# Sparse attention and a rational feed-forward layer on one core: two of nine chunks evaluate their polynomials from h squared and leave two sums to accumulating transfers, the magnitudes of b come later, and every engine has a new order

## The chip, the cores and the metric

One core of a Trainium2 chip. The metric is the device time of one execution in microseconds (us); the figure for a kernel is the median of its runs. The profile of one execution gives a span, from its first to its last instruction, and the time of that execution lies a little above its span.

## The reference, cut to what matters

Eight batches, eight heads, 576 positions, head dimension 64. Four heads see the last 32 positions, four see every 32nd position. The result x (4608 tokens by 512) goes through a layer whose activation is a quotient of polynomials:

```python
attn = softmax(where(mask[h], q @ k.T / 8, -1e9))
x = (attn @ v)                        # (4608, 512)
h = x @ w_in                          # (4608, 2048)
P = a[0] + a[1]*h + a[2]*h*h + a[3]*h*h*h
Q = 1.0 + abs(b[0])*abs(h) + abs(b[1])*h*h
out = (P / (Q + 1e-6)) @ w_out        # (4608, 512)
```

## The kernel before, in words

The program is one flat list of operations. `graph` records each of them with its tiles, `P.op` derives what it must wait for, and five lists of numbers, `ORDER`, say in which order each engine runs them; `AT` places the PSUM banks. Nothing is decided at run time. An engine works strictly down its list, so an instruction that waits holds up all that stand behind it in that list.

Attention runs batch by batch (`attention`, b = 0 to 7). GpSimd's queue casts q, k and v (`casts`), SyncE's queue loads and transposes them from batch 2 on (`loads`, L464 to L492), TensorE (PE) computes scores, VectorE (DVE) the row maxima and sums (L637, L666, L748), ScalarE (ACT) the exponentials (L661, L764, L767), and ACT evicts the result into XT, the transposed x (L413, called from L838 and L888). For batch 0 the sums of the strided softmax are L666, their reciprocal L668.

The feed-forward layer runs in nine chunks of 512 tokens (`mlp`, c = 0 to 8; the "chunks 7 and 8" of the change are c = 6 and 7 here). Per chunk, PE computes 16 blocks of 128 features (`w1`, L907), ACT evicts each into h (L918), and a group of up to 8 blocks, 128 x 4096 elements in bf16, is then evaluated at once:

- |h| into z, on ACT (L934) or on DVE (L938);
- Q: u = |b1|z + |b0| (L941), u = u z (L944), on DVE;
- 1/Q as exp(-ln(1 + u)), two halves each on ACT (L948, L953);
- P by Horner's rule in z on DVE: L957, L960, L962, L964, L966;
- h = z u (L968), on DVE.

PE then multiplies h by w_out (`w2`, L984), in pieces of four matmuls, ACT evicts (L992) and SyncE's queue stores (L998). Chunks 0 to 7 have groups of 8 blocks (chunk 0: 4, 4, 8), chunk 8 has 8, 4, 2, 2. The groups of a chunk are counted from 0, so "group 6,1" is the second of chunk 6. In the table MLP (L1033) chunk 6 has |h| on ACT in both groups, chunk 7 on ACT in its first and on DVE in its second.

The magnitudes |b0|, |b1| are one small DVE instruction (`babs`, L317) behind two small loads that ACT's queue issues (L314). Matmuls on constants (`fill`, L306) keep PE at work: 10 at the start, 5 in batch 0, 12 before the last products of chunk 8. Zeros are written by DVE (L327) and by ACT (L329), the latter as 0.0 times a column of the constants, which must have landed first.

## Time and profile before

| | |
|---|---|
| median of 3 runs | 373.1 us (367.28 to 377.19) |
| the profiled execution | 368.85 us, span 367.0 us, mean granted clock 0.963 |
| busy: PE, DVE, ACT | 324.5, 321.5, 318.8 us (88, 88, 87%) |
| busy: GpSimd (POOL) | 55.0 us (15%) |
| DMA engines | 0.5 to 1.0 busy up to about 240 us, then 0.0 to 0.2 in the slices of the page |

How to read it: three engines are equally busy over the whole, so the sums alone do not tell which bounds. What an engine waited for is in brackets behind a row of the timeline, with the wait in us. A row of the timeline merges neighbours of one kind ("x39"), and a row's duration includes the first instruction's start-up, so that two DVE or ACT instructions that follow each other overlap a little in these rows: what one costs in a full queue is the distance between the starts.

### The profile page before, as it was taken

The page shows a single profiled execution, that of the slowest core. Times are in us where ns is not written, and L with a number is a line of the kernel's source. Part 1 is how long each engine was busy: PE and PEld are TensorE (multiplying, and loading weights), DVE is VectorE, ACT ScalarE, POOL GpSimd, SP SyncE. Part 2 cuts the span into 40 slices and gives each one's busy share as a digit, 9 for nine tenths or more (in the row PEclk, how much of TensorE's full clock was granted, in tenths as well). Part 3 has the DMA queues.
Part 4 walks back from the last instruction along what each step waited for, and adds up shares of the span by engine and source line. Part 5 has one row for each costly group of instructions (what it writes and reads, how often), then busy time and mean ns, then how long its engine had stood idle before and what let it go on. Part 6 is the DMA issues. An engine that isn't in the chain of part 4 may idle for free.

```text
span 367.0 us, 9362 instructions
## 1 busy us (share of the span) xinstructions
PE 324.5 (88%) x4173; PEld 163.9 (45%) x4221; DVE 321.5 (88%) x272; ACT 318.8 (87%) x372; POOL 55.0 (15%) x90
## 2 busy tenths in 40 slices
PE   5669987779989995999999988999999799999795
PEld 2445544434544543445444544454454344444342
DVE  6961999998999995769998999799899969999991
ACT  7646798968999995599999999989999999999872
POOL 8893000240050014000600310000000000000000
PEclk9896999969999997899999999999999899999999
DMA  9999999688969959967999899810202010100202
GB/s 153 201 154 179 216 200 169 113 161 139 199 147 205 187 85 170 190 144 146 159 197 196 178 147 210 146 72 17 63 3 59 30 57 0 59 29 29 86 30 114
DMA packets 93080, 46.24 MB, mean 126 GB/s; under 512 B 79376, under 2 KB 86160, under 8 KB 92560
## 3 DMA queue, kind: packets, MB, share of 16 engines
q1 hardware_dynamic: 77168, 27.27, 38.1%
q0 software_dynamic: 14400, 18.07, 32.2%
q8 instruction: 33, 0.54, 0.6%
q10 hardware_dynamic: 1472, 0.30, 0.6%
q14 instruction: 7, 0.06, 0.1%
HBM read 38.58 MB, written 18.28 MB: 155 GB/s over the span
## 4 chain that ended last, share of the span: by engine, by line
ACT 40%; PE 31%; DVE 21%; issue 4%; DMA 3%; ACTq 0%
PE ps L907 14%; PE ps L984 12%; ACT u L948 10%; ACT u L953 8%; ACT h L918 8%; ACT z L934 6%; DVE u L944 3%; DVE z L960 3%; ACT XT L413 3%; DVE h L968 2%; DVE z L964 2%; DMA coef<-in_moe_a_dram 2%; DVE u L941 2%; DVE z L957 2%; ACT os L992 1%
## 5 line engine op out<-in xcount | busy, mean ns | idle before, releaser
L907 PE MATMUL ps<-XT,Win 128*128 128x512 bf16 x555 | 132.9, 386 | 8.1 <-ACT XT L413 5.5
L984 PE MATMUL ps<-Wout,h 128*128 128x512 bf16 x549 | 132.6, 386 | 6.3 <-issue 3.1
L918 ACT ACTIVATE h<-ps 128x512 bf16<-128x512 f32 x144 | 79.4, 622 | 16.5 <-PE ps L907 16.4
L907 PEld LDWEIGHTS ps<-XT,Win 128*128 128x128 bf16 x576 | 55.3, 99 | 72.5 <-issue 6.2
L984 PEld LDWEIGHTS ps<-Wout,h 128*128 128x128 bf16 x576 | 54.7, 99 | 66.8 <-issue 3.6
L948 ACT ACTIVATE u<-u 128x2048 bf16<-128x2048 bf16 (+1 forms) x40 | 68.7, 1751 | 1.7 <-DVE u L944 1.5
L953 ACT ACTIVATE u<-u 128x2048 bf16<-128x2048 bf16 (+1 forms) x40 | 69.5, 1759 | 0.1
L934 ACT ACTIVATE z<-h 128x2048 bf16<-128x2048 bf16 (+1 forms) x28 | 47.2, 1746 | 1.9 <-DVE h L968 1.7
L968 DVE TENSOR_TENSOR h<-z,u 128x4096 bf16<-128x4096 bf16 (+2 forms) x21 | 41.6, 1979 | 0.6
L944 DVE TENSOR_TENSOR u<-u,z 128x4096 bf16<-128x4096 bf16 (+2 forms) x21 | 41.6, 1983 | 0.4
L960 DVE TENSOR_TENSOR z<-z,h 128x4096 bf16<-128x4096 bf16 (+2 forms) x21 | 41.5, 1978 | 0.3
L964 DVE TENSOR_TENSOR z<-z,h 128x4096 bf16<-128x4096 bf16 (+2 forms) x21 | 41.5, 1976 | 0.3
L941 DVE TENSOR_SCALAR u<-z,coef 128x4096 bf16<-128x4096 bf16 (+2 forms) x21 | 24.8, 1180 | 7.5 <-ACT z L934 7.5
L400 POOL DMA_DIRECT2D vS<-in_v_dram x32 | 22.9, 722 | 37.6 <-DMA vL<-vL 27.3
L992 ACT ACTIVATE os<-ps 128x512 f32<-128x512 f32 x36 | 21.5, 627 | 7.1 <-PE ps L984 7.1
L957 DVE TENSOR_SCALAR z<-h,coef 128x4096 bf16<-128x4096 bf16 (+2 forms) x21 | 24.9, 1187 | 0.3
L966 DVE TENSOR_SCALAR z<-z,coef 128x4096 bf16<-128x4096 bf16 (+2 forms) x21 | 23.7, 1128 | 0.2
L962 DVE TENSOR_SCALAR z<-z,coef 128x4096 bf16<-128x4096 bf16 (+2 forms) x21 | 23.5, 1118 | 0.1
L413 ACT ACTIVATE XT<-ps 128x576 bf16<-128x576 bf16 (+5 forms) x36 | 20.2, 615 | 1.5 <-PE ps L882 1.4
L362 POOL DMA_DIRECT2D qk<-in_k_dram x12 | 6.3, 523 | 87.3 <-DMA vL<-vL 87.3
L803 PEld LDWEIGHTS ps<-ptS,vS 18*64 18x64 bf16 x896 | 9.1, 106 | 10.4 <-issue 6.4
L803 PE MATMUL ps<-ptS,vS 18*64 18x18 bf16 x896 | 11.4, 175 | 2.2 <-DVE xl L870 1.2
(95 smaller groups left out, 255.0 us busy)
## 6 DMA issues: line engine op xcount, KB each, us to landing
out_dram<-os SPq DMA_DIRECT2D x36, 256.0 KB, 2.2
qk<-in_q_dram POOLq DMA_DIRECT2D x12, 288.0 KB, 7.4
qk<-in_k_dram POOLq DMA_DIRECT2D x12, 288.0 KB, 6.9
vS<-in_v_dram POOLq DMA_DIRECT2D x32, 72.0 KB, 9.3
Win<-in_moe_w_in_dram POOLq DMA_DIRECT2D x2, 1024.0 KB, 12.6
Wout<-in_moe_w_out_dram POOLq DMA_DIRECT2D x2, 1024.0 KB, 20.9
v<-in_v_dram POOLq DMA_DIRECT2D x6, 288.0 KB, 7.6
vL<-v SPq DMA_DIRECT2D x24, 72.0 KB, 4.0
```

Of the source, the lines that this page charges most:

```text
L907: r = e.matmul(bank(ph, 0, CH), Win[:, kk, f * 128:(f + 1) * 128], XT[:, kk, c * CH % NR:c * CH % NR + CH], start=(kk == 0), stop=(kk == N ...
L918: P.op("act", lambda e, f=f, ph=ph, h=h, f0=f0: e.activation(h.t[:, f - f0, :], bank(ph, 0, CH), AF.Copy), "ev512", ("hev", c, f), r=[ph], ...
L934: P.op("act", lambda e, z=z, h=h, i=i, hp=hp: e.activation(z.t[:, hp * i:hp * i + hp, :], h.t[:, hp * i:hp * i + hp, :], AF.Abs), f"act_{h ...
L941: dv(lambda e, z=z, u=u, G_=G_: e.tensor_scalar(u.t[:, 0:G_, :], z.t[:, 0:G_, :], b1_ap, b0_ap, op0=Alu.mult, op1=Alu.add), "ts2", "u1", r ...
L944: dv(lambda e, z=z, u=u, G_=G_: e.tensor_tensor(u.t[:, 0:G_, :], u.t[:, 0:G_, :], z.t[:, 0:G_, :], op=Alu.mult), "tt", "u2", r=[z], m=[u])
L948: lns.append(P.op("act", lambda e, u=u, i=i, hp=hp: e.activation(u.t[:, hp * i:hp * i + hp, :], u.t[:, hp * i:hp * i + hp, :], AF.Ln, bias ...
L953: exs.append(P.op("act", lambda e, u=u, i=i, hp=hp: e.activation(u.t[:, hp * i:hp * i + hp, :], u.t[:, hp * i:hp * i + hp, :], AF.Exp, sca ...
L957: dv(lambda e, z=z, h=h, G_=G_: e.tensor_scalar(z.t[:, 0:G_, :], h.t[:, 0:G_, :], a_ap[3], a_ap[2], op0=Alu.mult, op1=Alu.add), "ts2", "p1 ...
L960: dv(lambda e, z=z, h=h, G_=G_: e.tensor_tensor(z.t[:, 0:G_, :], z.t[:, 0:G_, :], h.t[:, 0:G_, :], op=Alu.mult), "tt", "p2", r=[h], m=[z])
L964: dv(lambda e, z=z, h=h, G_=G_: e.tensor_tensor(z.t[:, 0:G_, :], z.t[:, 0:G_, :], h.t[:, 0:G_, :], op=Alu.mult), "tt", "p4", r=[h], m=[z])
L968: dv(lambda e, z=z, h=h, u=u, G_=G_: e.tensor_tensor(h.t[:, 0:G_, :], z.t[:, 0:G_, :], u.t[:, 0:G_, :], op=Alu.mult), "tt", "g", r=[z, u], ...
L984: r = e.matmul(bank(po, 0, Fout), h.t[:, j, m * 128:(m + 1) * 128], Wout[:, kk, :], start=(kk == 0), stop=(kk == NF - 1))
```

## The change

Four things are changed.

1. Chunks 6 and 7 (`ADDED`) are evaluated by `chain_added`. With t = |b0||h| (ACT takes the factor along as `scale`; DVE needs one more instruction) DVE computes u = h h, s = a3 h + a2, z = a1 h + a0, s = s u and u = |b1| u. The two sums u + t and z + s are made by `into`: a transfer from GpSimd's queue between tiles on chip that adds to its destination, one per sum and group, eight in all, 1 MB each (128 rows of 2 x 2048 elements). ln and exp on u and the product h = z u follow as before. s, t and a third u lie over the tiles of q, k and v, which are free after the attention of batch 7; both chunks are therefore recorded behind it.
2. `babs` is recorded after batch 0's attention and waits for its `lnorm` (L870 of before).
3. ACT's zeros are copied from a column of zeros that DVE writes, and no longer wait for the constants.
4. Fills: 6 behind the first turn of q, 8 behind `lneg` of batch 0 (5 before), 8 behind `snorm` of batch 0. And all five orders and the banks are new; of these tables the diff shows two lines.

```diff
-    QK = [sb(f"qkT{i}", [128, 3 * W]) for i in range(2)]
+    QK_ = sb("qkT", [128, 6 * W])
+    QK = [QK_[:, 3 * W * i:3 * W * i + 3 * W] for i in range(2)]
...
+    L = [Tile(f"l{i}", x[:, o:o + G * CH].rearrange("p (g c) -> p g c", g=G)) for i, (x, o) in enumerate(
+        ((QK_, 0), (VL_, 0), (VL_, NV2), (QK_, G * CH), (QK_, 2 * G * CH)))]
+    R_s, R_t, R_u3 = Ring(L[0:2]), Ring(L[2:4]), Ring(R_u.tiles + L[4:5])
...
+    def babs():
+        last = [o for o in P.ops if o.lab == ("lnorm", 0)]
         P.op("dve", lambda e: e.scalar_tensor_tensor(coef[:, 6:8], coef[:, 4:6], -1.0, coef[:, 4:6],
-                                                     op0=Alu.mult, op1=Alu.max), "tiny", ("babs",), r=[T_co], w=[T_b])
+                                                     op0=Alu.mult, op1=Alu.max), "tiny", ("babs",), r=[T_co], w=[T_b],
+             after=last)
...
+    P.op("dve", lambda e: e.memset(zc[:, :], 0.0), "tiny", ("zc",), w=[T_zc])
...
-            P.op("act", lambda e: e.activation(o(), src, AF.Copy, scale=0.0), kind, lab, r=[T_id], w=[t])
+            P.op("act", lambda e: e.activation(o(), src, AF.Copy), kind, lab, r=[T_zc], w=[t])
...
+                    if (b, nm, pair) == (0, "ql", 0):
+                        fill(6, 3, [o])
...
+        if two:
+            fill(8, 4, [o])
...
-            fill(5, 1, [o])
+            fill(8, 1, [o])
...
+    def into(dst, src, nm, c, gi):
+        if not hasattr(dst, "ac"):
+            dst.ac = Tile("a" + dst.name)
+        dst.ac.new()
+        W = G * CH
+        o = P.op("pool", lambda e: e.dma_start(dst.t.rearrange("p g c -> p (g c)"), src.t.rearrange("p g c -> p (g c)"),
+                                               accum_op=Alu.add, max_dma_last_dim=4096), "issue", (nm, c, gi),
+                 r=[src], w=[dst.ac], after=dst.prev + dst.w + dst.r, dma=(256, 300))
+        dst.w, dst.r = [o], []
...
+    def chain_added(c, gi, h, G_, on_act):
+        u, z, s, t = R_u3.next(), R_z.next(), R_s.next(), R_t.next()
...
+        if on_act:
+            for i in range(2):
+                P.op("act", lambda e, i=i: e.activation(t.t[:, 4 * i:4 * i + 4, :], h.t[:, 4 * i:4 * i + 4, :], AF.Abs,
+                                                        scale=b0_ap), f"act_{W // 2}", ("abs", c, gi, i), r=[h, T_b], w=[t])
+        else:
+            dv(lambda e: e.tensor_scalar(t.t.bitcast(u16)[:, :, :], h.t.bitcast(u16)[:, :, :], 0x7FFF, None,
+                                         op0=Alu.bitwise_and), "ts1", "absd", r=[h], w=[t])
+            dv(lambda e: e.tensor_scalar(t.t[:, :, :], t.t[:, :, :], b0_ap, None, op0=Alu.mult), "ts1", "u0", r=[T_b],
+               m=[t])
+        dv(lambda e: e.tensor_tensor(u.t[:, :, :], h.t[:, :, :], h.t[:, :, :], op=Alu.mult), "tt", "u1", r=[h], w=[u])
+        dv(lambda e: e.tensor_scalar(s.t[:, :, :], h.t[:, :, :], a_ap[3], a_ap[2], op0=Alu.mult, op1=Alu.add), "ts2", "p1",
+           r=[h, T_co], w=[s])
+        dv(lambda e: e.tensor_scalar(z.t[:, :, :], h.t[:, :, :], a_ap[1], a_ap[0], op0=Alu.mult, op1=Alu.add), "ts2", "p2",
+           r=[h, T_co], w=[z])
+        dv(lambda e: e.tensor_tensor(s.t[:, :, :], s.t[:, :, :], u.t[:, :, :], op=Alu.mult), "tt", "p3", r=[u], m=[s])
+        dv(lambda e: e.tensor_scalar(u.t[:, :, :], u.t[:, :, :], b1_ap, None, op0=Alu.mult), "ts1", "u2", r=[T_b], m=[u])
+        into(u, t, "ua", c, gi)
+        into(z, s, "za", c, gi)
...
+        dv(lambda e: e.tensor_tensor(h.t[:, :, :], z.t[:, :, :], u.t[:, :, :], op=Alu.mult), "tt", "g", r=[z, u], m=[h])
...
+            if c in ADDED:
+                chain_added(c, gi, h, G_, abs_act[gi])
+                groups.append((f0 - G_, G_, h))
+                continue
...
+        if b == 0:
+            babs()
...
+        if b == B - 1:
+            qs = [R.tiles[i] for R in (R_sqk, R_lq, R_lk) for i in range(2)]
+            L[0].over, L[3].over, L[4].over = qs, qs, qs
+            L[1].over, L[2].over = [R_vL.tiles[0]], R_vL.tiles[0:2]
-        while nxt < NCH and (nxt + 1) * CH <= (b + 1) * S:
+        while nxt < NCH and (nxt + 1) * CH <= (b + 1) * S and (nxt < ADDED[0] or b == B - 1):
...
+ADDED = (6, 7)
...
-        "20 13 21 11 26 12 24 19 29 23 27 22 31 34 14 30 33 69 32 72 86 75 65 90 93 79 92 142 82 125 151 49 "
+        "27 14 24 15 20 13 22 12 25 23 33 30 75 21 11 92 96 71 78 34 28 32 85 31 35 81 99 98 88 156 131 134 "
...
```

How the order moves, at the three places on which a number of the prediction rests. A row has the line, the operation, and output<-inputs with their buffer numbers; in the changed kernel the line numbers are its own.

DVE in the attention of batch 0, before: L317 is `babs`, L666 and L668 are the sum and the reciprocal of the strided softmax.

```order
L637 TENSOR_REDUCE ng0<-ps 128x32
L413 COPY ptL0<-ps 128x512
L317 SCALAR_TENSOR_TENSOR coef<-coef 128x2
L666 TENSOR_REDUCE rc0<-h1 128x32
L413 COPY qkT1<-ps 64x576
```

And now (L652 and L681 are the same two reductions, L324 is `babs`):

```order
L652 TENSOR_REDUCE ng0<-ps 128x32
L681 TENSOR_REDUCE rc0<-h1 128x32
L426 COPY ptL0<-ps 128x512
L683 RECIPROCAL rc0<-rc0 128x32
L684 TENSOR_TENSOR h1<-h1,rc0 128x2x16x18
L884 RECIPROCAL rc1<-ps 128x18
L887 TENSOR_TENSOR xl0<-ps,rc1 128x1152
L426 COPY h1<-ps 128x512 x2
L426 COPY qkT<-ps 128x576
L324 SCALAR_TENSOR_TENSOR coef<-coef 128x2
```

`babs` stood ahead of the sum; now it stands behind all of batch 0's normalizations.

ACT between chunk 6's first evictions and chunk 7's, before: L934 is |h| of chunk 6, L948 and L953 are ln and exp of its groups, L413 into XT are the evictions of batch 7, on which chunk 7's first matmul waits.

```order
L934 ACTIVATE z<-h 128x2048 x2
L948 ACTIVATE u<-u 128x2048 x2
L953 ACTIVATE u<-u 128x2048
L413 ACTIVATE XT<-ps 128x576
L953 ACTIVATE u<-u 128x2048
L992 ACTIVATE os<-ps 128x512
L948 ACTIVATE u<-u 128x2048 x2
L413 ACTIVATE XT<-ps 128x576 x2
L953 ACTIVATE u<-u 128x2048 x2
L918 ACTIVATE h<-ps 128x512
```

And now (L987 evicts into h, L1065 the output, L934 is |b0||h|, L952 and L956 are ln and exp, L426 evicts into XT):

```order
L934 ACTIVATE vL<-h,coef 128x2048 x2
L987 ACTIVATE h<-ps 128x512
L1065 ACTIVATE os<-ps 128x512
L426 ACTIVATE XT<-ps 128x576 x2
L1065 ACTIVATE os<-ps 128x512
L987 ACTIVATE h<-ps 128x512
L426 ACTIVATE XT<-ps 128x576
L987 ACTIVATE h<-ps 128x512
L426 ACTIVATE XT<-ps 128x576
L934 ACTIVATE qkT<-h,coef 128x2048 x2
L987 ACTIVATE h<-ps 128x512 x3
L952 ACTIVATE u<-u 128x2048
```

All four evictions of batch 7 now stand ahead of chunk 6's first ln; three evictions of chunk 7 do, too, and the rest of chunk 7's stand behind it.

DVE at the first group of chunk 6, now (L681 to L684 are batch 7's softmax; L941, L942, L944, L946, L947 are u, s, z, s and u of `chain_added`; L884 and L887 batch 7's last normalization):

```order
L681 TENSOR_REDUCE rc2<-pS0 128x32
L765 TENSOR_REDUCE ng3<-ps 128x18
L683 RECIPROCAL rc2<-rc2 128x32
L684 TENSOR_TENSOR pS0<-pS0,rc2 128x32x18
L944 TENSOR_SCALAR z1<-h1,coef 128x4096
L941 TENSOR_TENSOR u0<-h1 128x4096
L942 TENSOR_SCALAR qkT<-h1,coef 128x4096
L946 TENSOR_TENSOR qkT<-qkT,u0 128x4096
L884 RECIPROCAL rc3<-ps 128x18
L947 TENSOR_SCALAR u0<-u0,coef 128x4096
L887 TENSOR_TENSOR xl1<-ps,rc3 128x1152
```

Before, the group had eight instructions here, from L941 to L968; now the sum for z can be issued after L946 and that for u after L947, in this order on GpSimd's queue, behind the last casts:

```order
L413 DMA vS1<-in_v_dram 18x4x512 x4
L916 DMA z1<-qkT 128x2x2048
L916 DMA u0<-vL 128x2x2048
L916 DMA z0<-vL 128x2x2048
L916 DMA u1<-qkT 128x2x2048
L916 DMA qkT<-vL 128x2x2048
L916 DMA z1<-qkT 128x2x2048
L916 DMA u0<-qkT 128x2x2048
L916 DMA z0<-vL 128x2x2048
```

More of the change, by code (lines that the diff above doesn't have):

```diff
@@ L263, in graph @@
     T_sk = [Tile(f"skB{i}") for i in range(2)]
[L264 removed]
+    NV2 = 4 * NB * 65
+    VL_ = sb("vL", [128, 2 * NV2])
+    VL = [VL_[:, NV2 * i:NV2 * i + NV2] for i in range(2)]
     R_vL = Ring([Tile(f"vL{i}", VL[i][:, :].rearrange("p (a s m c) -> p a s m c", a=2, s=2, m=NB)) for i in range(2)])
```

36 lines of the change are left out of this document (28 added, 8 removed), and 113 rows, old and new, of the table ORDER.

## The prediction

> **What bounds the kernel now.** The change takes work from DVE in the last third, so I first cut the span there into stretches and read the busy time of each engine. T0 is the end of chunk 5's last product, from which on the two kernels differ in what DVE does.
>
> ```profile
> core 0: us, PE busy (x) PEld busy (x) DVE busy (x) ACT busy (x) POOL busy (x), PEclk, DMA share, GB/s
> 240.00:263.70 23.70, 23.33 (x277) 11.60 (x279) 23.44 (x15) 22.20 (x32) 0.00 (x0) 1.00 0.19 58
> 263.70:287.10 23.40, 20.03 (x378) 10.64 (x381) 21.39 (x18) 23.40 (x21) 0.00 (x0) 0.98 0.10 25
> 287.10:342.70 55.60, 55.30 (x247) 24.83 (x252) 52.51 (x33) 53.64 (x59) 0.00 (x0) 0.98 0.10 38
> 342.70:349.00 6.30, 3.60 (x18) 1.46 (x17) 6.30 (x6) 4.99 (x8) 0.00 (x0) 1.00 0.21 83
> 349.00:367.00 18.00, 13.91 (x63) 6.16 (x64) 10.40 (x18) 9.00 (x11) 0.00 (x0) 1.00 0.19 74
> ```
>
> From 287 to 343 us PE is busy for 55.30 of 55.60 us: nothing that DVE does faster can shorten that stretch. What is left are the stretches on its two sides. The timeline of PE shows the two waits in them, and the timelines of ACT and DVE what they waited for.
>
> ```profile
> 287.09 9.78 PE L907 MATMUL ps<-XT,Win 128*128 128x512 bf16 x39 [2.85 <-ACT XT L413]
> ...
> 298.43 5.34 PE L907 MATMUL ps<-XT,Win 128*128 128x512 bf16 x23
> ...
> 342.67 2.11 PE L306 MATMUL ps<-con 128*128 128x512 bf16 x9
> 344.61 1.03 PE L907 MATMUL ps<-XT,Win 128*128 128x512 bf16 x4
> 345.47 0.81 PE L306 MATMUL ps<-con 128*128 128x512 bf16 x3
> 348.98 13.99 PE L984 MATMUL ps<-Wout,h 128*128 128x512 bf16 x63 [2.70 <-DVE h L968]
> ```
> ```profile
> 281.80 3.76 ACT L948 ACTIVATE u<-u 128x2048 bf16<-128x2048 bf16 x2
> 285.40 1.24 ACT L413 ACTIVATE XT<-ps 128x576 bf16<-128x576 f32 x2
> 286.46 3.77 ACT L953 ACTIVATE u<-u 128x2048 bf16<-128x2048 bf16 x2
> ```
>
> The first wait, 2.85 us, is for two evictions into XT that stood behind two ln on ACT; the second, 2.70 us, for DVE's product of chunk 8's first group. Of the rest of PE's list there, the 12 constant matmuls are instructions that run in any case.
>
> **DVE's part.** In a full queue the distance between starts is the price.
>
> ```profile
> 261.43 2.29 DVE L968 TENSOR_TENSOR h<-z,u 128x4096 bf16<-128x4096 bf16 x1
> ...
> 281.21 2.28 DVE L964 TENSOR_TENSOR z<-z,h 128x4096 bf16<-128x4096 bf16 x1
> 283.41 1.34 DVE L957 TENSOR_SCALAR z<-h,coef 128x4096 bf16<-128x4096 bf16 x1
> 284.67 1.28 DVE L966 TENSOR_SCALAR z<-z,coef 128x4096 bf16<-128x4096 bf16 x1
> 285.87 2.28 DVE L960 TENSOR_TENSOR z<-z,h 128x4096 bf16<-128x4096 bf16 x1
> ...
> 300.23 1.35 DVE L941 TENSOR_SCALAR u<-z,coef 128x4096 bf16<-128x4096 bf16 x1 [2.64 <-ACT z L934]
> ...
> 346.64 2.28 DVE L968 TENSOR_TENSOR h<-z,u 128x4096 bf16<-128x4096 bf16 x1
> ```
>
> A product of two tiles costs 283.41 - 281.21 = 2.20 us, a two-step scaling 1.26, a one-step one 1.20; T0 = 261.43 + 2.20 = 263.6. A group of eight blocks had four products, two two-step and two one-step scalings: 8.80 + 2.52 + 2.40 = 13.7 us. It now has three, two and one: 6.60 + 2.52 + 1.20 = 10.3 us. Four groups save 4 x 3.4 = 13.6 us, less one scaling by |b0| of 1.20 in group 7,1: 12.4 us. The product for which PE waits at 346.64 to 348.98 is reached by a run of DVE work without another wait since 300.23, so DVE comes there early by most of 12.4 us, and the 2.70 us vanish: **-2.7 us**, and no more, since PE was full before.
>
> **The order's part.** The new list of ACT has batch 7's evictions ahead of chunk 6's first ln, so the 2.85 us vanish: **-2.85 us**. Behind that wait 39 matmuls took 9.78 us, 0.251 each, against 23 in 5.34, 0.232, and 63 in 13.99, 0.222; with no wait ahead I price them at 0.222, 39 x 0.029 = **-1.1 us**.
>
> **babs.** At the start DVE stood for 1.50 us at `babs`, for a load.
>
> ```profile
> 21.11 0.65 ACT L661 ACTIVATE h<-ps 128x576 bf16<-128x576 f32 x1 [1.00 <-PE ps L644]
> ...
> 22.79 0.16 DVE L317 SCALAR_TENSOR_TENSOR coef<-coef 128x2 f32<-128x2 f32 x1 [1.50 <-DMA coef<-in_moe_a_dram]
> 22.86 0.75 DVE L666 TENSOR_REDUCE rc<-h 128x32 f32<-128x576 bf16 x1
> ```
>
> The sum L666 behind it could have run when the exponential L661 ended, 21.11 + 0.65 = 21.76: it gains 22.86 - 21.76 = 1.1 us, and the normalization, XT and the first products follow it: **-1.1 us** (0 if the first products then wait for something else). ACT's zeros and the 17 more constant matmuls I count at nothing. The zeros move behind the first evictions, which wait for the casts' landing in any case; if they end on the path they cost what they cost now, four of 0.7 us, 2.8 us. The 17 matmuls at 0.222 us are 3.8 us of PE, in the first 60 us where PE has gaps; without that cover they cost the 3.8.
>
> **The transfers.** No transfer of before adds to its destination, and none of 1 MB runs on chip. The nearest rows:
>
> ```profile
> GB/s 0 0 0 0 0 0 0 100 213 10 0 0 0 0 0 103 54 0 0 157 0 0 0 0 9 148 0 157 157 10 114 43 0 0 0 0 23 133 295 175
> ...
> out_dram<-os SPq DMA_DIRECT2D x12, 256.0 KB, 2.1
> ```
> ```profile
> Win<-in_moe_w_in_dram POOLq DMA_DIRECT2D x2, 1024.0 KB, 12.6
> ```
>
> These are the stores in the last 67 us, alone on their engines, with the best slice at 295 GB/s, and the two 1 MB loads of GpSimd's queue at the crowded start. Bounds for what one transfer occupies: 1.049 MB / 295 GB/s = 3.6 us below, as if the second read cost nothing; 12.6 us above. If both tiles are read at that rate it is 7.1 us. I take 5.3, between 3.6 and 7.1, because the engines are as empty as in the store's row; and 2.1 us from the end of its turn to its landing, from that row.
>
> Now the first group (T0 = 0; DVE: three small ones and a reduction 2.9, scaling 1.26, product 2.2, scaling 1.26, product 2.2): the sum for z is issued at 9.8, the one for u, after L947, at 11.2. The queue is taken by the first until 15.1, by the second until 20.4, and u lands at 22.5. ACT's list up to that ln, by its rows:
>
> ```profile
> 255.88 0.33 ACT L771 ACTIVATE pL<-ps 128x128 bf16<-128x128 f32 x1
> 256.04 1.14 ACT L918 ACTIVATE h<-ps 128x512 bf16<-128x512 f32 x2
> 256.99 1.99 ACT L953 ACTIVATE u<-u 128x2048 bf16<-128x2048 bf16 x1
> 258.80 1.65 ACT L918 ACTIVATE h<-ps 128x512 bf16<-128x512 f32 x3
> 260.23 0.70 ACT L992 ACTIVATE os<-ps 128x512 f32<-128x512 f32 x1
> 260.70 2.67 ACT L918 ACTIVATE h<-ps 128x512 bf16<-128x512 f32 x5
> ```
>
> 19 evictions into h at 0.48, 4 of the output at 0.47, 4 of |h| at 1.8, and batch 7's seven small ones, about 3.7 by the 0.53 of an eviction into XT: 21.9 us after chunk 5's last exp. That exp ended at 258.8, 2.6 us ahead of the product that uses it; if the product follows at once it ends at -2.2, so ACT arrives between 17.1 and 19.7. I take the later, since DVE has less to do in front of that product now. ACT then stands for 22.5 - 19.7 = 2.8 us, with the 13 other evictions of chunk 7 behind it, which PE waits for as soon as its eight banks are full: **+2.8 us**. DVE's product of group 6,0, at 26 by DVE's list alone, waits for the exp, at about 34; those 8 us, with the work of 7,0 and 7,1 behind it, are covered by the 12.4. Bounds: at 3.6 us per transfer u lands at 19.1, no wait; at 7.1 it lands at 26.1, +6.4 (+9.0 with the earlier arrival); at 12.6 the whole queue decides, below.
>
> The Trainium skill, "DMA: Bandwidth & Descriptors", section "Anatomy of one DMA — SWDGE (gpsimd) path", fits 2.0 us plus the bytes at 436 GB/s to a plain transfer of this queue: an estimate of 2.4 us of occupation, by which u lands before ACT comes and the 2.8 us fall away. No row here shows 436 GB/s; the best slice has 295.
>
> **Sum**: -2.7 - 2.85 - 1.1 - 1.1 + 2.8 = -4.95, say -5.0 us. Against the profiled execution, 368.85, that is 363.9; the median of the runs shown is 4.25 us above that execution, so the forecast is 373.1 - 5.0 = **368.1 us**, which is 1.3% less. About 2%, 7.5 us, is what a measurement of this kernel can tell from no change, and its three runs lie 9.9 us apart.
>
> **Rivals.**
>
> *The transfers are slow, and the kernel is slower.* From the first issue the queue would never run empty: the last of eight lands at 9.8 + 8 S + 2.1 for S us each, and the last product of chunk 7 ends 2.2 later. ACT's own list, without waits, ends the exp that this product needs 47.9 us after ACT's arrival (eight ln and eight exp and four |h| at 1.8, 21 evictions into h, four of the output), so the product ends near 70. The queue decides from S = (70 - 14.1) / 8 = 7.0 us on, and has eaten the gain of 7.75 when S = 8.0. At 10, between 7.0 and the loads' 12.6, it ends at 94.1: +24.1 - 7.75 = +16 us, 389 us. For: 12.6 us is the only row for 1 MB on this queue. Against: those loads ran in the crowded first 45 us, and the DMA share after 264 us is 0.10.
>
> *The gain is eaten at ACT alone.* With S = 7.1 ACT's wait is 6.4 to 9.0 us: -7.75 + 7.7 = 0, 373 us.
>
> *The new order does more.* In the profiled execution PE lost time in the middle to no wait that the trace names:
>
> ```profile
> 143.57 0.54 PE L591 MATMUL ps<-qkT 64*18 64x18 bf16 x49 [4.01 <-issue]
> ...
> 140.00:160.00 20.00, 16.04 (x142) 7.36 (x144) 10.61 (x11) 11.85 (x17) 3.11 (x6) 0.83 1.00 184
> ```
>
> If the new lists do not meet this, 4.0 us of it go, and about the same again in what DVE and ACT then lack (10.6 and 11.9 of 20 us busy): with the ACT wait hidden too, 373.1 - 7.75 - 4.0 = 361 us, or down to 355 with the follow-on. Against: it names no cause that the change removes.
>
> *DVE locks GpSimd out.* DVE works on without a gap while GpSimd writes descriptors for 256 pieces per transfer.
>
> ```profile
> L362 POOL DMA_DIRECT2D qk<-in_k_dram x12: 486/514/622, 26.0 to 205.2; - x12
> L400 POOL DMA_DIRECT2D vS<-in_v_dram x20 | 14.9, 749 | 33.0 <-DMA vL<-vL 27.3 <-PE ps L803 5.7
> ```
>
> Were each of the first two issues held for one scaling, 1.26 us, ACT would wait 2.5 us longer: 370.6. The rows show a spread of 0.14 us between the shortest and the longest, at a DVE that is 88% busy over the span, so little of it. The Trainium skill, "SBUF — State Buffer", section "Who interferes with whom", says that a scaling in a two-port mode holds the shared pair for its whole length and that GpSimd blocks; by the 0.14 us the trace hardly agrees.
>
> **How the numbers follow.** The forecast and its neighbours within 2% (368, 371, 373): 0.22 for the forecast, 0.15 for the gain eaten at ACT, 0.05 for the lock, so 0.42 for same. Faster by over 2%, below 365.6: the ACT wait hidden (365.3) 0.20, the order's gain 0.18, so 0.38. Slower by over 2%, above 380.6: the queue, from S = 9 on: 0.18, and 0.02 of other mishaps of the order count there: 0.20. The range takes in the order's 355 and most of the slow queue, up to 386.
>
> **What would show it.** Right: PE without the waits ahead of chunk 7's first matmul and of chunk 8's products; DVE some 12 us less busy; `babs` without a wait; ACT standing 0 to 6 us at the first ln of group 6,0 for a transfer; transfers of 5 to 9 us from issue to landing. Wrong: transfers of over 10 us, PE idle in the middle of chunks 6 to 8, or a first product of chunk 0 no earlier than 30.7 us.

## The result, and the profile after

The changed kernel is slower: 378.9 us, median of four runs (377.0 to 379.8), against 370.2 for the kernel before (365.1 to 377.2); the ratio is 1.031, 95% interval 1.026 to 1.037. The forecast was 368.1 us and "within 2%". The profiled execution took 378.49 us with a span of 376.7 (before: 368.85 and 367.0). Medians here are of all runs, ratios leave disturbed executions out on both sides, and the profiled execution of before is one of the longer ones, with the excess ahead of T0, as shown further down.

T0 is again the end of chunk 5's last product, and I count from it to the end of the span. The first row is DVE's timeline of after, the others are the windows of before and of after from T0 on (same columns).

```profile
259.23 2.29 DVE L1041 TENSOR_TENSOR h<-z,u 128x4096 bf16<-128x4096 bf16 x1
```
```profile
core 0: us, PE busy (x) PEld busy (x) DVE busy (x) ACT busy (x) POOL busy (x), PEclk, DMA share, GB/s
263.60:367.00 103.40, 92.94 (x702) 43.17 (x711) 90.70 (x72) 91.12 (x97) 0.00 (x0) 0.98 0.12 44
```
```profile
261.40:376.70 115.30, 98.25 (x593) 43.63 (x600) 79.80 (x65) 96.51 (x105) 10.33 (x8) 0.96 0.53 115
```

T0 is at 259.23 + 2.20 = 261.4, 2.2 us earlier than in the profiled execution before, but the rest takes 115.3 us instead of 103.4. DVE is less busy, 79.8 instead of 90.7 us in this stretch, and 309.1 instead of 321.5 over the span: the 12.4 us of the forecast are there, 10.9 of them in this stretch. PE's timeline of after shows what it cost.

```profile
292.84 3.62 PE L976 MATMUL ps<-XT,Win 128*128 128x512 bf16 x16
298.16 3.63 PE L976 MATMUL ps<-XT,Win 128*128 128x512 bf16 x16 [1.71 <-ACT h L987]
...
315.17 6.03 PE L1057 MATMUL ps<-Wout,h 128*128 128x512 bf16 x16 [9.14 <-DVE h L960]
321.03 7.07 PE L976 MATMUL ps<-XT,Win 128*128 128x512 bf16 x31
...
359.30 14.20 PE L1057 MATMUL ps<-Wout,h 128*128 128x512 bf16 x62
```

The 2.85 us wait ahead of chunk 7's first matmul and the 2.70 us wait ahead of chunk 8's products are gone, as forecast. In their place PE stands for 9.14 us in the middle of the stretch in which it had been full, for the product of group 6,1; and the 16 matmuls behind that wait took 6.03 us, 0.377 each, where 16 took 3.62 before it. ACT's timelines, one row of before and then after, show why that product is late:

```profile
273.59 3.74 ACT L948 ACTIVATE u<-u 128x2048 bf16<-128x2048 bf16 x2
```
```profile
270.90 3.90 ACT L934 ACTIVATE vL<-h,coef 128x2048 bf16<-128x2048 bf16 x2
...
283.78 1.57 ACT L987 ACTIVATE h<-ps 128x512 bf16<-128x512 f32 x3
287.79 1.91 ACT L952 ACTIVATE u<-u 128x2048 bf16<-128x2048 bf16 x1 [2.43 <-DMA u<-vL]
...
305.00 3.81 ACT L952 ACTIVATE u<-u 128x2048 bf16<-128x2048 bf16 x2
308.60 3.80 ACT L956 ACTIVATE u<-u 128x2048 bf16<-128x2048 bf16 x2
...
313.99 3.71 ACT L952 ACTIVATE qkT<-qkT 128x2048 bf16<-128x2048 bf16 x2 [1.10 <-DMA qkT<-vL]
```

The first ln of chunk 6 starts at 287.79, 26.4 us behind T0, where before it started at 273.59, 10.0 behind T0. From then on ACT has hardly a gap, and the ln of group 6,1 comes 43.6 us behind T0 instead of 18.2. DVE, meanwhile, stands and waits, and its chain of chunk 8 starts late; these are rows of DVE's timeline, the products of groups 6,0 and 6,1 of before, then those of after with the first instruction of chunk 8:

```profile
288.07 2.28 DVE L968 TENSOR_TENSOR h<-z,u 128x4096 bf16<-128x4096 bf16 x1
...
295.30 2.29 DVE L968 TENSOR_TENSOR h<-z,u 128x4096 bf16<-128x4096 bf16 x1
```
```profile
299.93 2.29 DVE L960 TENSOR_TENSOR h<-z,u 128x4096 bf16<-128x4096 bf16 x1
...
312.83 2.28 DVE L960 TENSOR_TENSOR h<-z,u 128x4096 bf16<-128x4096 bf16 x1
...
335.58 1.34 DVE L1014 TENSOR_SCALAR u<-z,coef 128x4096 bf16<-128x4096 bf16 x1 [11.96 <-ACT z L1007]
```

The transfers themselves came near to what was forecast. These are the issues of GpSimd's queue at the first two (POOL's timeline, then the list of issues with the time to landing, of the second one and of the third, which had none ahead of it):

```profile
271.85 1.33 POOL L916 DMA_DIRECT2D z<-qkT  x1 [60.96 <-DVE rc L884]
275.38 1.22 POOL L916 DMA_DIRECT2D u<-vL  x1 [2.21 <-ACT h L987]
```
```profile
u<-vL POOLq DMA_DIRECT2D x1, 1024.0 KB, 12.4
z<-vL POOLq DMA_DIRECT2D x1, 1024.0 KB, 8.1
```

With none ahead of them the first, the third and the fifth landed 10.0, 8.1 and 8.4 us after their issue (forecast 7.4). The 2176 / 8 packets of one keep the 16 engines full for 5.9 us (38.4% of the 122 us from 255 to 377, for eight; forecast 5.3). ACT's wait at its first ln of chunk 6 was 2.43 us (forecast 2.8).

### The profile page after: what moved, and what is told of

Same layout as the page of the kernel before. It is cut to its first block, busy times and chain, and to the rows that moved or that the text cites. A ratio compares the mean times of both kernels' runs of the same rounds, so it can differ in the third digit from the quotient of the medians.

```text
span 376.7 us, 9397 instructions
## 1 busy us (share of the span) xinstructions
PE 332.3 (88%) x4189; PEld 164.3 (44%) x4238; DVE 309.1 (82%) x266; ACT 321.8 (85%) x372; POOL 66.4 (18%) x98
## 4 chain that ended last, share of the span: by engine, by line
DVE 32%; PE 31%; ACT 24%; DMA 7%; issue 5%; DVEq 0%; ACTq 0%
PE ps L976 13%; PE ps L1057 11%; ACT h L987 6%; ACT z L1007 5%; DVE u L1017 4%; ACT u L1021 3%; DMA u<-vL 3%; DVE z L1033 3%; ACT u L1026 3%; DVE z L1037 3%; DVE h L1041 3%; DVE u L1014 3%; DMA u<-qkT 3%; ACT XT L426 2%; DVE z L1035 2%
## 5 line engine op out<-in xcount | busy, mean ns | idle before, releaser
L987 ACT ACTIVATE h<-ps 128x512 bf16<-128x512 f32 x144 | 80.4, 611 | 14.3 <-PE ps L976 13.8
L1021 ACT ACTIVATE u<-u 128x2048 bf16<-128x2048 bf16 (+1 forms) x32 | 53.8, 1700 | 8.7 <-DVE u L1017 8.7
L1026 ACT ACTIVATE u<-u 128x2048 bf16<-128x2048 bf16 (+1 forms) x32 | 54.2, 1709 | 0.1
L1014 DVE TENSOR_SCALAR u<-z,coef 128x4096 bf16<-128x4096 bf16 (+2 forms) x17 | 19.5, 1147 | 22.8 <-ACT z L1007 22.8
L1007 ACT ACTIVATE z<-h 128x2048 bf16<-128x2048 bf16 (+1 forms) x22 | 36.0, 1684 | 0.2
L1041 DVE TENSOR_TENSOR h<-z,u 128x4096 bf16<-128x4096 bf16 (+2 forms) x17 | 32.4, 1908 | 0.5
L1033 DVE TENSOR_TENSOR z<-z,h 128x4096 bf16<-128x4096 bf16 (+2 forms) x17 | 32.5, 1911 | 0.2
L1037 DVE TENSOR_TENSOR z<-z,h 128x4096 bf16<-128x4096 bf16 (+2 forms) x17 | 32.4, 1904 | 0.2
L1017 DVE TENSOR_TENSOR u<-u,z 128x4096 bf16<-128x4096 bf16 (+2 forms) x17 | 32.4, 1905 | 0.1
L1065 ACT ACTIVATE os<-ps 128x512 f32<-128x512 f32 x36 | 21.1, 627 | 7.1 <-PE ps L1057 7.1
L426 ACT ACTIVATE XT<-ps 128x576 bf16<-128x576 bf16 (+5 forms) x36 | 19.8, 594 | 4.7 <-PE ps L899 3.5
L413 POOL DMA_DIRECT2D vS<-in_v_dram x32 | 22.1, 695 | 8.8 <-PE ps L820 4.7
L1030 DVE TENSOR_SCALAR z<-h,coef 128x4096 bf16<-128x4096 bf16 (+2 forms) x17 | 19.4, 1141 | 0.3
L1035 DVE TENSOR_SCALAR z<-z,coef 128x4096 bf16<-128x4096 bf16 (+2 forms) x17 | 18.5, 1091 | 0.4
L1039 DVE TENSOR_SCALAR z<-z,coef 128x4096 bf16<-128x4096 bf16 (+2 forms) x17 | 18.5, 1089 | 0.2
L820 PE MATMUL ps<-ptS,vS 18*64 18x18 bf16 x896 | 12.6, 177 | 5.9 <-issue 4.1
```

The costliest lines, as they stand in the source:

```text
L426: return lambda e: e.tensor_copy(o_(), i_()) if e_ == "dve" else e.activation(o_(), i_(), AF.Copy)
L987: P.op("act", lambda e, f=f, ph=ph, h=h, f0=f0: e.activation(h.t[:, f - f0, :], bank(ph, 0, CH), AF.Copy), "ev512", ("hev", c, f), r=[ph], ...
L1007: P.op("act", lambda e, z=z, h=h, i=i, hp=hp: e.activation(z.t[:, hp * i:hp * i + hp, :], h.t[:, hp * i:hp * i + hp, :], AF.Abs), f"act_{h ...
L1014: dv(lambda e, z=z, u=u, G_=G_: e.tensor_scalar(u.t[:, 0:G_, :], z.t[:, 0:G_, :], b1_ap, b0_ap, op0=Alu.mult, op1=Alu.add), "ts2", "u1", r ...
L1017: dv(lambda e, z=z, u=u, G_=G_: e.tensor_tensor(u.t[:, 0:G_, :], u.t[:, 0:G_, :], z.t[:, 0:G_, :], op=Alu.mult), "tt", "u2", r=[z], m=[u])
L1021: lns.append(P.op("act", lambda e, u=u, i=i, hp=hp: e.activation(u.t[:, hp * i:hp * i + hp, :], u.t[:, hp * i:hp * i + hp, :], AF.Ln, bias ...
```

## The experiments

**Theory L**: the latency of the transfers. **Theory O**: the new lists, whatever makes the sums. **Theory P**: PE's wait itself, through the rule that the last two blocks of an output wait for all groups. After the first runs I added **theory W**: the way from |h| to ln, DVE's part and the transfer's together, is what paces the last third, because ACT works its list in order; what DVE is relieved of is worth nothing. The table has all 14 runs, with T0 (start of chunk 5's last product + 2.20) and the rest of the span behind it.

| run | kernel | median us | ratio to before, 95% | T0 | T0 to end |
|---|---|---|---|---|---|
| before | | 370.2 | 1 | 263.6 | 103.4 |
| after | | 378.9 | 1.031 (1.026-1.037) | 261.4 | 115.3 |
| e1 | after, sums by DVE | 392.6 | 1.065 (1.053-1.077) | 268.1 | 125.3 |
| e2 | after, u's sum first | 377.5 | 1.031 (1.025-1.037) | 261.3 | 112.8 |
| e3 | after, output blocks earlier | 380.8 | 1.038 (1.031-1.046) | 263.1 | 115.9 |
| e4 | before's lists, transfers | 423.0 | 1.153 (1.141-1.165) | 259.5 | 158.6 |
| e5 | after, no sums | 375.5 | 1.027 (1.018-1.037) | 263.5 | 110.3 |
| e6 | before's lists, new chain, no sums | 373.7 | 1.019 (1.004-1.035) | 268.9 | 109.4 |
| e7 | before, babs later | 373.5 | 0.997 (0.990-1.005) | 272.5 | 102.4 |
| e8 | before, evictions ahead | 369.8 | 1.007 (1.001-1.013) | 268.8 | 107.7 |
| e9 | before, less for DVE | 365.0 | 0.997 (0.992-1.001) | 259.7 | 103.3 |
| e10 | after, new lists at the end | 378.0 | 1.032 (1.024-1.039) | 263.8 | 110.7 |
| e11 | before, new lists at the end | 366.9 | 0.999 (0.993-1.006) | 263.4 | 102.9 |
| e12 | old chain, lists made anew | 415.8 | 1.133 (1.121-1.145) | 309.2 | 100.6 |
| e13 | e10, transposed read ahead | 374.3 | 1.011 (1.005-1.018) | 263.5 | 106.8 |
| e14 | e6, shorter way to ln | 371.4 | 0.998 (0.986-1.011) | 258.7 | 105.4 |

T0 and the rest are from one profiled execution of each kernel. T0 itself differs by 10 us among kernels with before's lists ahead of it (258.7 to 268.9; 272.5 with `babs` moved). Behind T0 e7, which changes nothing there, has 102.4 us for before's 103.4: PE's wait ahead of chunk 7 is 2.45 us instead of 2.85, and the clock granted to PE in the 5 us around its end is 1.00 instead of 0.66, so that 40 matmuls behind it take 8.90 us where 39 took 9.78. The stretch behind T0 therefore tells two kernels apart from about 1 us on; it is the better measure for a change that begins there.

### e1: the sums on DVE

```
-        o = P.op("pool", lambda e: e.dma_start(dst..., src..., accum_op=Alu.add, ...
+        o = P.op("dve", lambda e: e.tensor_tensor(dst, dst, src, op=Alu.add), ...
```


> The changed kernel with its new lists, but the eight sums of two tiles are made by DVE (one product-sized instruction each, 2.20 us) right behind the scaling that feeds them; GpSimd's eight transfers are gone. Theory L (latency: ACT's list cannot pass its first ln of chunk 6 until a transfer has landed, and what is lost there is never given back): ACT's waits for transfers, 2.43 us at 287.79, 1.10 at 313.99 and 1.01 at 326.29, vanish, so -4.5 us, 374 us; DVE's 17.6 us more fit into its own waits in that stretch (5.47, 6.03, 3.76 and 11.96). Theory O (order: the new lists cost the time, PE's 9.14 us wait above all, whatever makes the sums): 378 to 381 us, and PE still waits 7 us or more for the product of group 6,1.

Neither came: 125.3 us behind T0. The experiment is spoilt by where I put the first sum, ahead of batch 7's last normalization (L887): DVE stood there for |b0||h|, and PE for DVE. PE's timeline of e1:

```profile
287.38 0.29 PE L896 MATMUL ps<-con,xl 128*128 128x128 bf16 x1 [5.84 <-DVE xl L887]
```

It says nothing on L or O: DVE still has 19.5 us of waits behind T0, but not at the places where its list has the sums.

### e2 and e3: the queue's order, and PE's rule

GpSimd's list of e2 against after's, and e3's edit:

```
+L916 DMA u<-vL 128x2x2048
 L916 DMA z<-qkT 128x2x2048
-L916 DMA u<-vL 128x2x2048
```
```
-MLP = ... [([8, 8], [1, i % 2], 2) for i in range(7)] ...
+MLP = ... [([8, 8], [1, i % 2], 4 if i == 5 else 2) for i in range(7)] ...
```


> The changed kernel with one edit: in the two groups of chunk 6 GpSimd's queue sends the sum for u ahead of the sum for z, so the u of group 6,0 has no transfer in front of it. Theory L: it is issued at 274.8, when |b0||h| is written, and lands 8.4 us later, at 283.2, ahead of ACT's arrival at 285.4; the 2.43 us wait goes, 376.5 us. Theory O: no change, 378 to 380 us.

> The changed kernel, lists as they are, but the last two blocks of chunk 6's output may start before group 6,1's product is written. PE then has 16 matmuls (3.5 us) and up to four blocks of chunk 8's first matmul (3.5 us) to do in the 9.14 us for which it waited at 306 to 315 us. Theory P (PE's wait is itself the loss, 9.14 us and 2.5 us of slow matmuls behind it): 370 to 372 us. Theory L (ACT, which has no idle time of over 1.2 us from its first ln of chunk 6 to 350 us, sets the end, and PE's wait is only a consequence): 376.5 to 378.5 us, since ACT waited for PE there only 1.1 us at 322 to 325 us.

e2: u's sum is issued at 275.29 and lands 8.6 us later, ACT's ln starts at 285.11 without a wait, and the stretch behind T0 is 2.5 us shorter, as L says; the medians differ by 1.4, and the ratios to before are the same 1.031, so the gain rests on the profiled execution. PE still waits 9.14 us for group 6,1. PE's timeline of e2, and of e3:

```profile
312.52 5.36 PE L1057 MATMUL ps<-Wout,h 128*128 128x512 bf16 x16 [9.14 <-DVE h L960]
```
```profile
304.23 5.35 PE L1057 MATMUL ps<-Wout,h 128*128 128x512 bf16 x24 [0.60 <-ACT h L987]
314.77 3.60 PE L1057 MATMUL ps<-Wout,h 128*128 128x512 bf16 x8 [5.19 <-ACT os L1065]
323.67 7.90 PE L976 MATMUL ps<-XT,Win 128*128 128x512 bf16 x28 [3.59 <-ACT os L1065]
```

In e3 PE does the 16 matmuls earlier, and then stands 5.19 + 3.59 us for two evictions that sit behind ln and exp in ACT's list. Nothing is gained (115.9, and a median above both P's and L's range): P falls. The 9.14 us were ACT's lateness, shown at PE.

### e4: the transfers in the old lists

```
 # before's ORDER; DVE's places u1 u2 p1 p2 p3 of a group now hold
+# h*h, a3*h+a2, a1*h+a0, (a3*h+a2)*h*h, |b1|*h*h; p4 and p5 are gone
+# GpSimd's list ends with the eight transfers
```


> The kernel before with its own lists, where only the chains of chunks 6 and 7 are replaced by the new ones with eight transfers, each instruction in the place of the old one nearest to it. Theory L: ACT comes to its first ln of chunk 6 at 273.6, DVE has the u for the transfer at about 280, it lands 8 us later; ACT stands some 15 us with batch 7's XT evictions and chunk 7's behind it, so 380 to 390 us. Theory O (the transfers are innocent, the new lists cost the time): 365 to 371 us.

423 us, worse than L's 380 to 390, because each of the four groups pays (the last 10.4 us), not the first alone. ACT's timeline of e4 has the first three:

```profile
285.59 3.71 ACT L942 ACTIVATE u<-u 128x2048 bf16<-128x2048 bf16 x2 [14.02 <-DMA u<-vL]
305.18 3.71 ACT L942 ACTIVATE u<-u 128x2048 bf16<-128x2048 bf16 x2 [11.27 <-DMA u<-qkT]
345.40 3.71 ACT L942 ACTIVATE qkT<-qkT 128x2048 bf16<-128x2048 bf16 x2 [17.62 <-DMA qkT<-vL]
```

So O falls as well: the transfers are not innocent, and the new lists are what keeps the new chain from costing 50 us. That the new lists lose time of their own is not ruled out by this (e5, e13).

### e5 and e6: no sums at all

```
     def into(dst, src, nm, c, gi):
-        ... dma_start(..., accum_op=Alu.add, ...)
+        dst.w = dst.w + src.w
```


> The changed kernel without its eight transfers: the two sums of tiles in chunks 6 and 7 are left out of the computation (ln reads the scaled h squared alone, the product reads a0 + a1 h alone), so that a sum costs neither time nor latency; the lists are the new ones. Theory L alone (all that was lost is the latency of the transfers): the 12 us come back, 367 us or less. Theory LO (the latency costs only what ACT stood for it, 2.43 + 1.10 + 1.01 us; the rest lies in the new lists, which put group 6,0's |h| at 13.3 us behind chunk 5's last product instead of 3.5, and ln 13 us behind that): 379 - 4.5 = 374 us, and PE still waits some 7 us for group 6,1's product.

> The kernel before with its own lists, and in chunks 6 and 7 the new chain with the two sums left out of the computation and h squared scaled right behind the product that needs it unscaled. DVE is relieved of all that the transfers could take from it, and nothing lands late. The prediction's claim (the relief is worth the 2.70 us wait for group 8,0 and no more, PE being full from 287 to 343): 365 to 369 us where the kernel before takes 367 to 370. If DVE's load were what holds this kernel: 12 us less, 355 to 358. If even without a transfer the new chain's longer way to ln (four instructions, 6.9 us, instead of two, 3.5 us) costs more than the relief: over 370.

e5 agrees with theory LO: 110.3 us, 5.0 of the 11.9 lost come back, and PE still waits 8.92 us for group 6,1 (the ratios of e5 and after, 1.027 and 1.031, do not tell them apart: e5's T0 is 2.1 us later). e6 is the surprise: no transfer, the old lists, 12 us less for DVE, and yet 6 us more behind T0 than before. Its ACT waits for the scaled h squared, now the fourth of DVE's instructions instead of the second, and once for PE's read of a tile of vL that |b0||h| has to overwrite:

```profile
270.38 3.89 ACT L917 ACTIVATE vL<-h,coef 128x2048 bf16<-128x2048 bf16 x2 [1.74 <-PE ps L863]
...
290.17 3.71 ACT L935 ACTIVATE u<-u 128x2048 bf16<-128x2048 bf16 x2 [0.70 <-DVE u L930]
...
316.60 3.71 ACT L935 ACTIVATE qkT<-qkT 128x2048 bf16<-128x2048 bf16 x2 [3.81 <-DVE qkT L930]
```

### e7 and e8: two terms of the sum alone

```
+    def babs():      # called behind batch 0's attention
+        last = [o for o in P.ops if o.lab == ("lnorm", 0)]
         P.op("dve", ... ("babs",), r=[T_co], w=[T_b], after=last)
```
```
+L413 ACTIVATE XT<-ps 128x576 x2
 L948 ACTIVATE u<-u 128x2048 x2
-L413 ACTIVATE XT<-ps 128x576 x2
```


> The kernel before with the magnitudes of b computed behind the first batch's normalization, nothing else. The prediction's term: DVE's 1.50 us wait goes, the first matmul of chunk 0 starts 1.1 us earlier than 30.67, at 29.6, and the end comes 1.1 us earlier. Rival: the first matmul of chunk 0 moves, but the end does not, since something later (PE's stall of 4 us in the middle, or the waits at the end) takes it up: 0.

> The kernel before with one move in ACT's list: batch 7's last two evictions into XT ahead of the two ln of group 6,1, behind which they stood. The prediction's term: PE's 2.85 us wait at 287.09 and the slower 39 matmuls behind it go, -2.85 - 1.1 = -4 us. Rival: the evictions wait for PE's own matmuls of batch 7, which end at 284.2, so ACT stands there instead of computing ln; ln, exp and the product of group 6,1 come up to 2.5 us later, and chunk 7 no earlier: 0 to +2.5 us.

e7's first matmul of chunk 0 starts at 27.85; but in seven profiles with before's place of `babs` it started between 27.91 and 30.67, and in four of these `babs` did not wait at all: the 1.50 us were the load's landing in one execution. The ratio leaves room for the 1.1 us and for nothing. e8 is the rival's outcome: 0.7% slower, some 2.6 us (the stretch behind T0 is 4.3 us longer, but 1.7 of them are its last 64 matmuls, which took 15.67 us where 63 took 13.99, the clock being 0.86 in 350 to 360 us of that execution). The wait moved to ACT and came back to PE. ACT's timeline of e8, then PE's:

```profile
289.48 1.19 ACT L413 ACTIVATE XT<-ps 128x576 bf16<-128x576 f32 x2 [2.41 <-PE ps L803]
```
```profile
290.73 4.49 PE L907 MATMUL ps<-XT,Win 128*128 128x512 bf16 x20 [1.37 <-ACT XT L413]
298.55 6.18 PE L907 MATMUL ps<-XT,Win 128*128 128x512 bf16 x20 [3.33 <-ACT h L918]
```

### e9: the relief alone

```
+            if c not in (6, 7):
                 dv(... "tt", "p4", r=[h], m=[z])
                 dv(... "ts1", "p5", m=[z])
```


> The kernel before where in chunks 6 and 7 two of DVE's instructions per group are left out of the computation (the last product by h and the last addition of the polynomial), so that DVE has 4 x 3.4 = 13.6 us less to do there, as the change gives it, and nothing else differs: the way from |h| to ln, ACT's and PE's lists are the old ones. The prediction's term: the 2.70 us wait for group 8,0 goes, -2.7 us. If DVE's load holds the kernel: -10 us or more. Theory W (ACT's list in its order paces the last third; DVE's freed time turns into waits for ACT, and the product of group 8,0 comes when ACT has given |h| of chunk 8): 0 to -1 us, and DVE shows some 12 us more of waits for ACT.

The clearest run. The windows of e9 from T0 on (columns as above), its waits of DVE in that stretch, and those of the kernel before:

```profile
259.70:363.00 103.30, 92.89 (x702) 43.14 (x710) 77.25 (x64) 90.87 (x97) 0.00 (x0) 0.98 0.12 44
```
```profile
DVE u L941 <- ACT z L934: 10.7, 3, 7.8
DVE h L969 <- ACT u L953: 5.5, 2, 3.7
DVE rc L867 <- PE ps L856: 1.3, 1, 1.3
DVE ng L637 <- PE ps L591: 0.5, 1, 0.5
```
```profile
DVE u L941 <- ACT z L934: 2.6, 1, 2.6
DVE rc L867 <- PE ps L856: 1.4, 1, 1.4
DVE ng L637 <- PE ps L591: 0.5, 1, 0.5
```

DVE works 13.4 us less (77.25 for 90.70) and waits 13.5 us more (18.0 for 4.5). The stretch takes 103.3 us for 103.4, and PE's wait for group 8,0 is still 2.67 us:

```profile
344.96 13.99 PE L985 MATMUL ps<-Wout,h 128*128 128x512 bf16 x63 [2.67 <-DVE h L969]
```

### e10 to e13: better lists for the new chain, and for the old

e10 has after's instructions in new lists from about 235 us on; e13 is e10 with one move on DVE; e11 and e12 apply such lists to the old chain.

```
 e13 against e10, DVE:
+L681 TENSOR_REDUCE rc<-pS 128x32
+L683 RECIPROCAL rc<-rc 128x32
+L684 TENSOR_TENSOR pS<-pS,rc 128x32x18
 L884 RECIPROCAL rc<-ps 128x18
 L946 TENSOR_TENSOR qkT<-qkT,u 128x4096
 L947 TENSOR_SCALAR u<-u,coef 128x4096
-L681 TENSOR_REDUCE rc<-pS 128x32
-L683 RECIPROCAL rc<-rc 128x32
-L684 TENSOR_TENSOR pS<-pS,rc 128x32x18
```


> The changed kernel with the same instructions and the same eight transfers, but with new lists for the last 140 us: group 6,0's |h| earlier against chunk 5's last product, u's sum ahead of z's on GpSimd's queue, ACT's evictions of chunk 7 in the time that a transfer needs, group 6,1's product at 42 us behind chunk 5's last product instead of 53.6. Theory W (what the change lost, 115.3 us from chunk 5's last product to the end instead of 103.4, lies in how the lists carry the longer way to ln): 103 to 107 us for that stretch, 366 to 371 us in all, about level with the kernel before. Rival (the transfers slow whatever runs beside them, in any order): 110 us or more, 374 us or more.

> The re-listed transfers of e10 with one move on DVE: the sum, reciprocal and normalization of batch 7's short softmax ahead of the product and the scaling that feed the first transfer, so that the transposed read of its result is issued ahead of that transfer. If the transfer's hold on the DMA engines was the cause: that read lands in 3 us instead of 8.3, PE's 3.76 us and ACT's 3.75 us at 281 us go, and the stretch behind chunk 5's last product takes 106 to 108 us instead of 110.6, although u's transfer starts 1.7 us later. If the read was late for another reason, or the transfers slow more than that: 110 us or more.

e10 missed W's 103 to 107 and came out as its rival said: 110.7. Its PE stood 3.76 us in front of batch 7's product with ptS, a tile that a transposed read on chip writes. Timelines of SP, POOL and PE of e10, and the issue with its time to landing in e10 and in e13:

```profile
272.83 2.20 SPq L569 DMA_TRANSPOSE ptS<-pS  x1
```
```profile
271.37 1.28 POOL L916 DMA_DIRECT2D u<-vL  x1 [60.71 <-DVE u L947]
```
```profile
281.22 0.30 PE L820 MATMUL ps<-ptS,vS 18*64 18x18 bf16 x16 [3.76 <-issue]
```
```profile
ptS<-pS SPq DMA_TRANSPOSE x1, 8.3
```
```profile
ptS<-pS SPq DMA_TRANSPOSE x1, 2.7
```

The read was issued 1.5 us behind a transfer and landed at 281.1, 1 us behind that transfer (271.37 + 8.7 = 280.1). From 273 to 277.5 us no packet of SyncE's queue moves, from 277.5 to 279 us 47 do, and about 1000 small ones follow up to the landing. Issued ahead of the transfer, in e13, the read landed in 2.7 us; PE's wait is gone, and the end came 3.9 us earlier (106.8, ratio 1.011 for 1.032), as expected for the transfer's hold on the DMA engines. The Trainium skill, "DMA: Bandwidth & Descriptors", section "Queues, rings and completion order", says that a DMA engine takes turns between the queues that have work, a whole packet of typically 9 to 17 descriptors at a time. A transfer here has 2176 / 8 / 16 = 17 of the profile's packets on each engine, so, if one of these is a descriptor, its whole share can be one such turn, and the late read does not speak against the page.

> The kernel before, the same instructions, with lists of the last 140 us re-ordered in the same way as in the run above, without the new chain. If re-ordering alone is worth something here: 101 us instead of 103.4 from chunk 5's last product to the end, -2 us, 368 us at a time before of 370. If the old lists are at their best: 0.

> The changed kernel's start and its lists up to chunk 5 (zeros and magnitudes of b later, the new order of attention and the first products), with the old chain in chunks 6 and 7 and lists of the last 140 us near those of the kernel before. The part ahead of chunk 5's last product took 261.4 us in the changed kernel's profiled execution and 263.6 before: if that is the order's gain, and the tail is the old 103.4 or a little less, 3 to 5 us less than before, 365 to 367 us. If the first part's gain was chance: level with the kernel before.

e11 is level with before. e12 is a failure of my own lists ahead of T0 (its T0 is at 309); behind it 100.6 us show only that the lists there are not worse. Whether after's lists ahead of T0 are worth anything is answered by the table: T0 is at 261.3 to 268.1 in the five profiles that have them (middle one 263.1), and at 258.7 to 268.9 in the seven with before's (middle one 263.4). No gain is to be seen.

### e14: the way to ln alone

```
-        z-product (s*u), then u scaled by |b1|
+        u scaled by |b1|, then the product s*h
```


> As e6 (the kernel before with its own lists; new chain in chunks 6 and 7; both sums left out of the computation, no transfer), but h squared is scaled right behind its product, so that ln waits for two instructions of DVE (3.4 us) as in the old chain, not for four (6.9 us); the product into the odd part takes h in place of h squared, at the same cost. DVE does the same work as in e6. Theory W (the way to ln is what the new chain costs): the stretch behind chunk 5's last product falls from 109.4 back to 103 to 105 us. Rival (the new chain costs in another way, in its other tiles or in |b0||h|): 108 us or more.

W's outcome, 0.4 us outside its range: 105.4 us for 109.4, and 0.998 of the time before for 1.019, with the same work for DVE (309.4 and 309.3 us). The intervals of the two ratios still overlap, so the 4.0 us rest on the profiled executions. The first ln of the four groups, in us behind T0 (from ACT's timelines), set against the end:

| kernel | 6,0 | 6,1 | 7,0 | 7,1 | end |
|---|---|---|---|---|---|
| before | 10.0 | 18.2 | 40.7 | 50.2 | 103.4 |
| e14 | 12.0 | 20.3 | 42.8 | 52.4 | 105.4 |
| e6 | 12.2 | 21.2 | 47.7 | 56.3 | 109.4 |
| after | 26.4 | 43.6 | 52.6 | 64.9 | 115.3 |
| e5 | 23.8 | 41.0 | 48.6 | 59.9 | 110.3 |
| e13 | 17.9 | 33.0 | 46.3 | 62.6 | 106.8 |

In e14 and e6, which have before's lists, the end is later by what the last ln is later, to 0.2 us (2.0 for 2.2, 6.0 for 6.1). With other lists that does not hold: in after the ln of 7,1 is 14.7 late and the end 11.9, in e5 9.7 and 6.9, in e13 12.4 and 3.4. So W is shown for before's lists; in the new ones the way to ln is one part, and what ACT does between the ln is another. e5, which has no transfer, has its first ln only 2.6 us earlier than after: most of that lateness is the list and the way, not the landing.

No version beat the kernel before beyond the intervals; the best one that makes the sums by transfers, e13, is 1.1% slower.

## Why the prediction was wrong, point by point

- **DVE's saving** was right in size (12.4 us) and wrong in worth. The step "DVE comes there early by most of 12.4 us, and the 2.70 us vanish" took DVE's row without a wait since 300.23 for a run that would start earlier and stay without waits. e9 shows that the freed time turns into waits for ACT, 13.5 us of them, and that group 8,0's product comes no earlier. Term: 0 instead of -2.7.
- **The order's part**, -2.85 and -1.1: the wait vanished in after, but not as a gain. Moved alone (e8) the evictions cost 0.7%, because they wait for PE and hold up ln. The -1.1 came from one execution in which PE's clock fell at that wait; e7 has the wait and 40 matmuls in 8.90 us, 0.222 each. A wait that is named at PE was ACT's choice between two things that were both due.
- **babs**, -1.1: unresolved between 0 and 1.1 (e7). The price came from one execution of a load whose landing varies. In after the first matmul of chunk 0 starts at 28.98, within the range of before's place.
- **The transfers**: occupation 5.9 for 5.3, landing 8.1 to 10.0 for 7.4, ACT's wait 2.43 for 2.8. The mechanism was right and the occupation near, but that the wait fits is luck: u landed 26.4 us behind T0 instead of 22.5, and ACT came at 23.9 instead of 19.7. u's sum was issued at 14.0 instead of 11.2, because it waits for ACT's |b0||h| as well, where the prediction went by DVE's list alone. The queue, as a rival, did not decide, in line with its threshold of 7.0 us. By the 2.0 us plus bytes at 436 GB/s that the prediction cites from the Trainium skill, "DMA: Bandwidth & Descriptors", section "Anatomy of one DMA — SWDGE (gpsimd) path", an estimate of 4.4 us, the landing would have been about half of what was measured. DVE did not lock GpSimd out by the 1.26 us priced: the eight issues took 1.20 to 1.60 us, and the three of them that fell into a wait of DVE 1.20 to 1.23.
- **The step that failed** is "DVE's product of group 6,0, at 26 by DVE's list alone, waits for the exp, at about 34; those 8 us, with the work of 7,0 and 7,1 behind it, are covered by the 12.4". A delay that comes through ACT is not covered by time that DVE has. The product came at 38.5 behind T0 (24.5 before), and I stopped at 6,0: the one that PE needed next was 6,1, 51.4 behind T0 instead of 31.7, and PE had nothing else ahead of it in its list. The sum also priced ACT's wait for the transfer (2.4 of the 11.9) but not the way ahead of it: the new chain scales h squared only behind the product that reads it unscaled, 6.9 us of DVE instead of 3.5, then the transfer, 12.4 us from issue to landing; and ACT reached that ln at 23.9 behind T0 instead of the 19.7 forecast, since it idled 4.2 us for PE's matmuls into h, which the new list has later (|b0||h| of 6,0 is done 13.4 us behind T0; before, |h| was at 3.5).
- "Nothing that DVE does faster can shorten that stretch" was right; what I missed is that PE being full there, 55.30 of 55.60 us, says nothing of how much lateness it can stand. Before, the product of group 6,1 was done at 297.6, and the next run of output matmuls that could use it started at 303.61: a margin of at least 6.0 us (an estimate from DVE's and PE's timelines of before), against a product that came 19.7 us later.

What stays open: how the 11.9 us divide. Without sums 5.0 come back (e5); with better lists 8.5 of them come back behind T0 though T0 itself is then 2.1 later (e13); the two are one way seen at two places and do not add up. Also open is what the execution waits for ahead of T0 (below).

## What to carry to other kernels

Before work is moved from an engine, leave that work out and look: if its busy time turns into waits of its own, the engine only follows, and a relief buys nothing. Then measure the way from the operand to the first instruction of the engine that does set the pace, in time and not in work: a transfer that costs no engine anything still stands in that way with 8 us or more, and an in-order list passes the delay on to everything behind it. A wait shown at one engine may be another's lateness; moving the waiting work (e3, e8) moves the wait.
